# The order of a recorded kernel set anew: local attention and a long convolution on one core

## The chip, the cores and the metric

The kernel runs on one core of a Trainium2 chip. The time is the device time of one execution in microseconds (us), the median of several runs. The profile is one profiled execution, whose span (first to last instruction) is a little shorter than its time.

## What is computed

Two layers over 2048 positions of 576 channels, in bf16, their outputs side by side (1152 channels):

```python
# A: sliding dilated attention, 32 heads of 18 channels, 8 taps, dilation 2
qkv = x @ wqkv
logits[h,s,w] = q[h,s] . k[h,s-2w] * 18**-0.5     # where s-2w >= 0, else -1e9
o = sum_w softmax_w(logits)[h,s,w] * v[h,s-2w]
a = o @ wo
# B: H3 convolution
k_shift[t] = sum_{j<4} k[t-3+j] * shift_k[:, j]
kv = k_shift * v
y = irfft(rfft(pad(kv)) * rfft(pad(ssm_k)))[:2048]   # long causal convolution over time
b = q * (y + kv * ssm_D)
out = concat([a, b], axis=-1)
```

## The kernel before

**How the work is cut.** Everything lives on chip; the two layers are woven into each other. The convolution's transforms are matrix products: the 2048 positions of kv and of the filter are cut into four blocks, each is folded about its middle, multiplied by tables of cosines and sines, multiplied with the filter's spectrum, summed over pairs of blocks and brought back by the inverse tables. The attention projects x to q, k and v by five groups of channels, multiplies q with k shifted by a tap, sums over a head's channels with a matrix of ones, takes the softmax, spreads the weights over the channels by DMA, multiplies with v, and projects with wo.

**What sets the order.** Every piece of work is a job, a function under a short name in the dictionary `jobs`. The scheduler leaves the order alone: the last lines of the kernel (L1090 and L1091) take the names in the string ORDER (L19 to L36) one by one and record each job's instructions. Each engine and each DMA queue then works off its own instructions in the order in which they were recorded, and waits on semaphores for data and for buffers. So ORDER is the order of all engines' queues at once. A name with an apostrophe records a projection with its last channels (the tails) first. PSUM is cut into four slots (`slots`, `banks`, L103 on): a job takes the slot that was given back longest ago, and gives it back, for the order of recording, when its copy out has been recorded. On the chip TensorE waits until that copy is done.

**The names** that the text uses, with their lines in before:

- loads on SyncE's queue: load_x (L178), load_w (L137, L139), load_k (L194, L197, a block of k into a buffer `kj`), load_v (L203, L204, into `vt`), turn_x (L234, L235), Lf0 to Lf3 (the filter, by a transposing DMA, L211), Lk and Lv (k and v of later blocks), Fr (first rows, L578); D0 to D5 spread weights (L789)
- spread_taps (TensorE L449, ScalarE L452 into `skb`): the four taps of shift_k laid out over the partitions
- the tables' angles (VectorE L376, L377) and sines (ScalarE L378)
- turning a quarter of x (TensorE L406, its last 64 channels L411; copies on VectorE L464 and ScalarE L465, L476, tails L416), and project_first (TensorE L435, L437, ScalarE L439)
- T0 to T3: taps of one block (VectorE L513, L516, times v L532). M: folding (TensorE L541, ScalarE L544). k, q and v with two digits or three: projections (TensorE L320, L324, L331, L337, ScalarE L353)
- F: folding the filter (TensorE L598, ScalarE L601, a DMA of POOL's queue L603). K: filter units (TensorE L563, L564, ScalarE L614). x with three digits: the same for kv (L676, L678)
- L: products of q and k (VectorE L700); G: their sums (TensorE L714, ScalarE L718); RG (VectorE L774); sm: softmax (VectorE L738 to L750); V: weights times v (VectorE L808); A: their sums (TensorE L819, L833, ScalarE L822); O: the projection with wo (TensorE L883, L875, ScalarE L889)
- ak and ax: third sums for the product by three multiplications (VectorE L937); p: products of spectra (VectorE L945); z: their sums (TensorE L964, ScalarE L977, for z323 in part VectorE L975); i: inverse (TensorE L999, ScalarE L1002; the last, i3384L, L1018 and L1020); b: back (TensorE L1048, L1027, ScalarE L1054); Q: q's loads on POOL's queue (L927, L929); g: gates (VectorE L1064, the last ones L1009)

**The head.** Until the first name of ORDER, the kernel records its start by plain code: loads of x, k, v and weights, the spread of the taps, four tables, the turning of quarters 0 and 1 of x, and the four project_first.

Of the kernel before, what the change touches and what calls it, by code (L numbers as in the profile page):

```python
# [11 lines left out]
ACT = mybir.ActivationFunctionType  # L12
# [4 lines left out]
PSUM = bass.MemoryType.PSUM  # L17

ORDER = """  # L19
    T0 k00a k00b S1 k01a' k01b I0 k02a k02b k03a' I1 k03b X5 q10a q10b q11a' q11b Lk2 Lv2 T1 q12a q12b M00 q13a'  # L20
    Lk3 Lv3 Lf3 Lf2 Lf1 Lf0 Lw Lo3 Lo2 Lo1 Lo0 Fr Ex T2 q13b k10a k10b M10 k11a' k11b k12a k12b M01 k13a' k13b
    T3 N3 N2 M11 q24a q24b M20 k24a' k24b M21 F3 F2 M30 K310 K311 K312 K313 M31 SV Z2 x000 L000 L001 G000 G001
    L002 N1 N0 L003 x001 x010 F1 G002 G003 L004 L010 x011 K300 K301 K302 G004 G010 L011 L012 K303 K210 K211 K212
    K213 F0 G011 G012 L013 L014 K200 K201 K202 K203 U3 G013 G014 L100 RG0 RG1 sm0a K110 K111 K112 K113 x020 K100
    K101 K102 K103 U2 K010 x021 x030 K011 sm0b L101 K012 K013 v24a v24b G100 G101 L102 K000 K001 K002 K003 sm0c
    L103 G102 G103 sm0d D0 L104 L110 x031 v00a v00b v01a' G104 G110 L111 L112 v01b v02a v02b G111 G112 L113 L114
    v03a' v03b x200 x201 G113 G114 D1 D2 Wl U1 V04 v10a v10b A04 sm1a v11a' sm1b V10 V11 v11b v12a v12b sm1c
    x210 x211 x220 x221 A10 V12 sm1d D3 V13 D4 v13a' v13b x230 A11 V20 V21 x231 x100 x101 x110 x111 A20 V22 V23
    x120 x121 x130 x131 x300 A21 V34 A34 D5 V40 V41 x301 x310 x311 x320 x321 x330 x331 A40 V42 V43 O000 O001'
    A41 V50 V51 O010 O011' A50 V52 V53 O100 O101' A51 Tx2 Tk2 Q0 Q1 ak00 ax00 p000 ak01 ax01 p010 ak02 ax02 p020  # L30
    O110 z000 ak10 p100 O111' O020 z010 ax10 p101 O021' O030 z020 p110 p111 O031' O120 z100 z101 p120 p121 i000
    i02880 z110 z111 p200 p201 i001 i02881 b00 z120 z121 p202 p210 p211 b0288 O121' z200 z201 z202 g0 Q2 p212
    p220 p221 i100 i12880 i101 i12881 b10 z210 z211 z212 p222 ak30 p300 b1288 O130 O131' z220 z221 z222 g1 Q3
    p301 p302 ax30 p303 i200 i22880 i201 z300 z301 p310 p311 z302 z303 p312 p313 i22881 z310 z311 p320 p321 b20
    b2288 z312 z313 p322 p323 g2 i300 z320 z321 i301 z322 z323 b30 i3384L g30 g3384
"""  # L36

LHOMES = (0, 1, 2, 0, 1, 2, 0, 1, 2, 0, 1, 2, 0, 1, 0, 1, 0, 1, 0, 1)
# [11 lines left out]
def kernel(  # L50
# [121 lines left out]

    def kTok(m):
        return view(Ks, k_at(m, 2), [[D, 4], [1, D]])
    kjs, vts = [], []

    def load_x(qtr):
        nc.sync.dma_start(xnat[:, qtr], xf[512 * qtr:512 * qtr + 512, :].rearrange("(sb p) c -> p sb c", p=128))  # L178

    load_x(0)  # L180

    def load_k(i):

        eng = nc.sync
        kj = sp1.tile([128, 7, D], BF16, name="kj", bufs=2)
        r0 = BL * i
        low = [(0, 64)]
        if i == 0:
            nc.gpsimd.memset(kj[0:1, 0:3, :], 0.0)
            nc.gpsimd.dma_start(kj[0:1, 3:7, :], kf[0:4, :].unsqueeze(0))  # L190
            low = [(1, 49), (49, 64)]
        for a, b in ((3, 7), (0, 3)) if i == 0 else ((0, 7),):
            for p0, p1 in low:
                eng.dma_start(kj[2 * p0:2 * p1:2, a:b], bass.AP(  # L194
                    tensor=kf.tensor, offset=kf.offset + (r0 + 4 * p0 - 3 + a) * D,
                    ap=[[4 * D, p1 - p0], [D, b - a], [1, D]]))
            eng.dma_start(kj[1:128:2, a:b], bass.AP(tensor=kf.tensor, offset=kf.offset + (r0 + 256 + 3 - a) * D,  # L197
                                                    ap=[[4 * D, 64], [-D, b - a], [1, D]]))
        kjs.append(kj)

    def load_v(i):
        vt = sp1.tile([128, 4, D], BF16, name="vt", bufs=2)
        nc.sync.dma_start(vt[0:128:2], vf[BL * i:BL * i + 256, :].rearrange("(p c) d -> p c d", c=4))  # L203
        nc.sync.dma_start(vt[1:128:2], bass.AP(tensor=vf.tensor, offset=vf.offset + (BL * i + 256 + 3) * D,  # L204
                                              ap=[[4 * D, 64], [-D, 4], [1, D]]))
        vts.append(vt)

    def load_filter(m):

# [18 lines left out]
    load_w(nc.sync, 0)  # L228
    load_x(1)
# [150 lines left out]
    def table_k(c):  # L380
        return table(n_all[:, 2 * c:2 * c + 2, :], TK[:, c, :, :], n_all[:, 8, :], (2 + c, 2 + c), 2048, (256.0, 1792.0))
# [74 lines left out]
    spread_taps(512)  # L456
    spread_taps(0)
    sines = [table_k(0), table_k(1)]
    pts, held = zip(*[banks("ps_x", BF16) for _ in range(2)])
    for n in range(2):  # L460
        transpose_x(0, pts[n], 2 * n, range(4))
    tail_x(0, pts[1])
    for n in range(2):
        nc.vector.tensor_copy(xT(n, 0, 512), pts[0][:, n, 0:512])  # L464
        nc.scalar.activation(xT(2 + n, 0, 512), pts[1][:, n, 0:512], ACT.Copy)  # L465
    copy_tail(0, pts[1])
    slots.extend(held)
    spread_taps(256)
    sines += [table_x(0), table_x(1)]
    project_first(0, 0)  # L470
    pts, held = zip(*[banks("ps_x", BF16) for _ in range(2)])
    for n in range(2):
        transpose_x(1, pts[n], 2 * n, range(4))
    tail_x(1, pts[0])
    for n in range(2):
        nc.scalar.activation(view(xw, 3 * HB + 2048 * n + 512, [[1024, 2], [1, 512]]), pts[n][:, :, 0:512], ACT.Copy)  # L476
    copy_tail(1, pts[0])
    slots.extend(held)
    project_first(0, 2)
    sines[2]()  # L480
    for n in range(2):
        project_first(1, 2 * n)
        sines[3 - 3 * n]()
    def job(name, fn, *args):

        assert name not in jobs
        jobs[name] = partial(fn, *args)

    project(0, 1)
    project(0, 2)  # L490
    for jj in range(3):
# [142 lines left out]
    for m in range(NBL):  # L634
        job(f"N{m}", negate, m)
        job(f"F{m}", fold_filter, m)
        for cs in range(2):
            for gi in range(4):
                job(f"K{m}{cs}{gi}", filter_unit, m, cs, gi)
        if m:  # L640
            job(f"U{m}", turn_filter, m)
        if m > 1:
            job(f"Lk{m}", load_k, m)
# [479 lines left out]
```

## Time and profile before

| | us |
|---|---|
| median of 3 runs | 210.41 (210.32 to 210.48) |
| profiled execution, its own time | 210.57 |
| its span | 208.9 |
| TensorE busy | 200.0 (96%) |
| VectorE busy | 197.2 (94%) |
| ScalarE busy | 150.5 (72%) |
| POOL busy | 69.7 (33%) |

The granted clock of TensorE is 0.999. 'PE' is TensorE's matmuls, 'PEld' its loads of weights, DVE is VectorE, ACT is ScalarE, SPq the DMA queue of SyncE. A row of the timeline has the start, the busy time from there, the engine, the line and operation, out<-in, how many instructions the row joins, and in brackets the idle time just before with what ended it. A row of the groups has the busy time, the mean ns of one, and the idle time before them.

### The profile page before, as it was taken

To read this page: it belongs to the slowest core of one execution; us is meant where nothing else is said; L and a number is where in the kernel's file an instruction comes from. 1 tells how busy PE (TensorE), PEld (TensorE's weight loads), DVE (VectorE), ACT (ScalarE), POOL (GpSimd) and SP (SyncE) were. 2 spreads that over 40 slices of the span, in tenths; PEclk is the share of its full clock that TensorE was granted. 3 is DMA by queue.
4 is the path that set the end of the run, shared out by engine and by line. 5 is a ranking of instruction groups with operands and counts; after the bars stand their busy time and mean duration, and the time that the engine had idled before them with its cause. 6 is when DMAs were issued, how large, how long until landed. Compare 5 with 4: busy or idle time off the path is not lost.

```text
span 208.9 us, 5092 instructions
## 1 busy us (share of the span) xinstructions
PE 200.0 (96%) x2114; PEld 111.5 (53%) x2122; DVE 197.2 (94%) x150; ACT 150.5 (72%) x218; POOL 69.7 (33%) x104
## 2 busy tenths in 40 slices
PE   7999999999999999999999999999999999999891
PEld 2553344444655567453445465755566667676460
DVE  7989999999999999989899999999999999899982
ACT  3689866967898989965469687954588896764640
POOL 8999992023295095220280000004330001211000
PEclk9999999999999999999999999999999999999999
DMA  6999999999386466999999795789991105454034
GB/s 195 288 295 279 186 283 389 187 215 287 94 113 82 63 82 103 182 172 217 205 238 216 140 242 126 125 208 256 228 287 68 61 3 169 116 169 116 3 108 118
DMA packets 34084, 36.12 MB, mean 173 GB/s; under 512 B 17459, under 2 KB 28847, under 8 KB 34062
## 3 DMA queue, kind: packets, MB, share of 16 engines
q1 hardware_dynamic: 26380, 23.11, 44.7%
q0 software_dynamic: 5216, 10.19, 25.3%
q10 hardware_dynamic: 2466, 2.51, 3.6%
q8 instruction: 16, 0.26, 0.5%
q14 instruction: 6, 0.05, 0.1%
HBM read 13.11 MB, written 4.72 MB: 85 GB/s over the span
## 4 chain that ended last, share of the span: by engine, by line
PE 78%; DVE 10%; issue 5%; ACT 4%; DVEq 0%
PE ps_proj L320 16%; PE ps_wo L883 7%; PE ps_acc L819 6%; PE ps_z L964 6%; PE ps_fx L676 6%; PE ps_inv L999 5%; PE ps_fk L563 4%; PE ps_proj L435 3%; PE ps_log L714 3%; PE ps_proj L331 3%; PE ps_proj L324 3%; DVE qk L945 2%; DVE av L700 2%; PE ps_fk L564 2%; PE ps_fold L541 2%
## 5 line engine op out<-in xcount | busy, mean ns | idle before, releaser
L320 PE MATMUL ps_proj<-xw 128*128 128x512 bf16 x153 | 36.2, 380 | 0.7 <-issue 0.6
L700 DVE TENSOR_TENSOR av<-qk 128x4096 bf16<-128x4096 bf16 (+1 forms) x16 | 31.4, 2012 | 0.0
L320 PEld LDWEIGHTS <-xw 128*128 128x128 bf16 x160 | 14.3, 98 | 19.5 <-issue 4.3
L977 ACT ACTIVATE av<-ps_z 128x768 bf16<-128x768 f32 x23 | 17.4, 809 | 6.2 <-PE ps_z L964 6.2
L678 ACT ACTIVATE xw<-ps_fx 128x576 bf16<-128x576 f32 x32 | 18.9, 676 | 1.8 <-PE ps_fx L676 1.6
L353 ACT ACTIVATE qk<-ps_proj 128x1024 bf16<-128x1024 f32 x14 | 14.3, 1023 | 7.7 <-PE ps_proj L331 4.1
L945 DVE TENSOR_TENSOR qk<-xw,Ks 128x2304 bf16<-128x2304 bf16 x14 | 18.6, 1354 | 1.0 <-PE ps_z L964 0.7
L614 ACT ACTIVATE Ks<-ps_fk 128x576 bf16<-128x576 f32 x32 | 18.9, 718 | 0.8 <-PE ps_fk L564 0.6
L513 DVE TENSOR_TENSOR tB<-kj,skb 128x4608 bf16<-128x4608 bf16 (+1 forms) x8 | 19.3, 2417 | 0.1
L883 PE MATMUL ps_wo<-qk 128*128 128x288 bf16 x128 | 17.9, 287 | 0.0
L676 PE MATMUL ps_fx<-xw,TB 128*128 128x288 bf16 x128 | 17.8, 286 | 0.1
L563 PE MATMUL ps_fk<-Ks,TB 128*128 128x384 bf16 x62 | 16.2, 326 | 0.0
L999 PE MATMUL ps_inv<-av,TI 128*128 128x288 bf16 (+1 forms) x112 | 15.6, 292 | 0.6 <-ACT av L977 0.6
L819 PE MATMUL ps_acc<-av,ident 64*64 64x512 bf16 x160 | 15.3, 379 | 0.0
L564 PE MATMUL ps_fk<-Ks,TB 128*128 128x192 bf16 x62 | 15.2, 246 | 0.0
L676 PEld LDWEIGHTS <-TB 128*128 128x128 bf16 x128 | 12.0, 98 | 5.9 <-issue 2.5
L927 POOL DMA_DIRECT2D TB<-in_B_q_dram x4 | 3.0, 738 | 36.3 <-DVE v L945 23.5
L353 ACT ACTIVATE v<-ps_proj 128x1024 bf16<-128x1024 f32 x9 | 9.2, 1039 | 7.8 <-PE ps_proj L320 4.3
L883 PEld LDWEIGHTS <-qk 128*128 128x128 bf16 x128 | 11.5, 98 | 6.3 <-issue 3.8
L822 ACT ACTIVATE qk<-ps_acc 128x1024 bf16<-128x1024 f32 x8 | 8.2, 1023 | 8.0 <-PE ps_acc L819 8.0
L808 DVE TENSOR_TENSOR av<-Ks,v 128x4096 bf16<-128x4096 bf16 x6 | 13.7, 2287 | 0.0
L622 POOL DMA_DIRECT2D Ks<-Ks x7 | 11.1, 2100 | 7.1 <-ACT Ks L614 6.6
(194 smaller groups left out, 464.6 us busy)
## 6 DMA issues: line engine op xcount, KB each, us to landing
Ks<-Ks POOLq DMA_DIRECT2D x7, 576.0 KB, 8.7
TB<-av SPq DMA_DIRECT2D x12, 256.0 KB, 4.5
kj<-in_B_k_dram SPq DMA_DIRECT2D x6, 504.0 KB, 6.3
vt<-in_B_v_dram SPq DMA_DIRECT2D x8, 288.0 KB, 5.2
Ks<-av SPq DMA_DIRECT2D x8, 256.0 KB, 5.8
out_dram<-qk ACTq DMA_DIRECT2D x5, 288.0 KB, 3.1
Ks<-in_A_x_dram SPq DMA_DIRECT2D x2, 576.0 KB, 5.3
xw<-in_A_wqkv_dram SPq DMA_DIRECT2D x2, 576.0 KB, 6.1
```

The costliest lines, as they stand in the source:

```text
L320: nc.tensor.matmul(ps[:, jp, :], wq(kb, comp, 128 * ct, 128), xT(kb, 1024 * jj + 512 * jp, 512), **se)
L353: nc.scalar.activation(view(t, o + pad + 1024 * jj, [[512, 2], [1, 512]]), ps[:], ACT.Copy)
L513: tt(to, view(kj, row * D, [[D, n], [D, 4], [1, D]]), view(skb, row * D, [[D, n], [0, 4], [1, D]]), ALU.mult)
L563: nc.tensor.matmul(o[:, 0:2], w, rhs[:, 0:2], start=start, stop=stop)
L564: nc.tensor.matmul(o[:, 2], w, rhs[:, 2], start=start, stop=stop)
L614: nc.scalar.activation(view(Ks, k_at(m, cs ^ (m & 1)) + 96 * gi, [[768, 3], [384, 2], [1, 96]]), acc3(ps), ACT.Copy, scale=(PSG, MSG)[cs][ ...
L676: nc.tensor.matmul(ps[:, pm, 0:HD], TX[:, 2 * pm + c, 128 * gi:128 * gi + 128], kv[:, 2 * c + pm, HD * h:HD * h + HD], start=(c == 0), sto ...
L700: tt(view(P, at, [[step, 4], [256, nj], [1, 256]]), view(t, o + 256 * hh, [[0, 4], [512, nj], [1, 256]]), view(tk, ok + 2 + 8 * ug + 256 * ...
L819: nc.tensor.matmul(acc[64 * o:64 * o + 64, h, :], ident[64 * h:64 * h + 64, 64 * h:64 * h + 64], view(P[s], 256 * u, [[2048, 2], [1, 256]] ...
L883: nc.tensor.matmul(ps[:, r, 0:HD], oT(hh, j + 2 * r, t)[:, o:o + 128], wo[:, t // 2, t % 2, HD * h:HD * h + HD], start=(t == 0 and not fli ...
L945: tt(product_home(n), view(xw, HB * XG[i] + QTR * t, [[HB, 3], [1, QTR]]), view(Ks, k_at(j - i, 0) + QTR * t, [[HB, 3], [1, QTR]]), ALU.mult)
L999: nc.tensor.matmul(ps[:, c, 0:n], TI[:, sl, pm, 128 * c:128 * c + 128], Yall(j % 2, pm, sl, slice(c0, c0 + n)), start=(pm == 0 and sl == 0 ...
```

## The change

Three things. The head's work becomes jobs: spread_taps (`sp0`, `sp256`, `sp512`), the tables' angles (`ta0` to `ta3`) and sines (`S0`, `S2`, `S3`, beside S1), the turning of quarter q by halves n (`tqn`), project_first (`pfqn`), and the loads (`LXn`, `LWn`, `LTn`, `Lk0a`, `Lk0b`, `Lvn`, `Lk1`). The kj of block 0 is cleared and its first row loaded on POOL's queue behind the making of `ident`. And ORDER is a new string, from its first name to its last. The number of instructions of each engine stays.

```diff
-    load_x(0)
-    def load_k(i):
+    def load_k(i, part):
...
-    for a, b in ((3, 7), (0, 3)) if i == 0 else ((0, 7),):
+        a, b = ((3, 7), (0, 3), (0, 7))[part]
...
+    kjs[0] = sp1.tile([128, 7, D], BF16, name="kj", bufs=2)
+    nc.gpsimd.memset(kjs[0][0:1, 0:3, :], 0.0)
+    nc.gpsimd.dma_start(kjs[0][0:1, 3:7, :], kf[0:4, :].unsqueeze(0))
...
-    load_k(0)
-    load_w(nc.sync, 1)
-    load_v(0)
-    load_k(1)
-    turn_x(0)
-    turn_x(1)
-    load_v(1)
...
+    def turn_quarter(qtr, n):
+        pt, slot = banks("ps_x", BF16)
+        transpose_x(qtr, pt, 2 * n, range(4))
+        tail = n != qtr
+        if tail:
+            tail_x(qtr, pt)
+        if qtr == 0:
+            for e in range(2):
+                if n:
+                    nc.scalar.activation(xT(2 + e, 0, 512), pt[:, e, 0:512], ACT.Copy)
+                else:
+                    nc.vector.tensor_copy(xT(e, 0, 512), pt[:, e, 0:512])
+        else:
+            nc.scalar.activation(view(xw, 3 * HB + 2048 * n + 512, [[1024, 2], [1, 512]]), pt[:, :, 0:512], ACT.Copy)
+        if tail:
+            copy_tail(qtr, pt)
+        slots.append(slot)
```

ORDER begins in before `T0 k00a k00b S1 k01a' k01b I0`, and in after `LX1 ta0 LX0 sp256 t10 ta2 sp0 sp512 t11 t01 t00 LW0 pf11 Lk0a pf10 Lk0b pf00 LW1 S0 k02a k00a Lk1 ta1 pf01 k03a' Lv0 LT0 ta3 k03b T0`. Quarter 1 is now loaded and turned first.

Where the instructions stand, at three places. ScalarE at the start, behind the load of its tables (`ps_sk` are spread taps, `ps_x` turned x, `ps_proj` projections), in before:

```order
L452 ACTIVATE skb<-ps_sk 128x4x64
L452 ACTIVATE skb<-ps_sk 128x4x256
L465 ACTIVATE xw<-ps_x 128x512 x2
L416 ACTIVATE xw<-ps_x 64x512
L452 ACTIVATE skb<-ps_sk 128x4x256
L439 ACTIVATE qk<-ps_proj 128x2x512
L476 ACTIVATE xw<-ps_x 128x2x512 x2
L416 ACTIVATE xw<-ps_x 64x512
```

and in after:

```order
L440 ACTIVATE skb<-ps_sk 128x4x256
L474 ACTIVATE xw<-ps_x 128x2x512
L404 ACTIVATE xw<-ps_x 64x512
L440 ACTIVATE skb<-ps_sk 128x4x256
L440 ACTIVATE skb<-ps_sk 128x4x64
L474 ACTIVATE xw<-ps_x 128x2x512
L470 ACTIVATE xw<-ps_x 128x512 x2
L404 ACTIVATE xw<-ps_x 64x512
L427 ACTIVATE qk<-ps_proj 128x2x512 x3
```

All copies of turned x now come ahead of the first projection's, with the spread of sp0 and sp512 between the first half of quarter 1 and the rest. On VectorE the copies of t00 stand behind two of the four tables (ta0 and ta2) and ahead of the others, as the copies of quarter 0 did in before.

VectorE in the middle, at the products of weights and v (L808); the last row below is the first product with the weights that D5 spreads into TB. The difference, + for after:

```order
 L808 TENSOR_TENSOR qk<-qk,v 128x4096
+L937 TENSOR_TENSOR xw<-xw 128x768
 L808 TENSOR_TENSOR av<-TB,v 128x4096
+L937 TENSOR_TENSOR xw<-xw 128x768
+L937 TENSOR_TENSOR Ks<-Ks 128x768 x2
+L937 TENSOR_TENSOR xw<-xw 128x768
 L808 TENSOR_TENSOR av<-Ks,v 128x4096
 L808 TENSOR_TENSOR qk<-Ks,v 128x4096
 L808 TENSOR_TENSOR av<-Ks,v 128x4096 x2
 L808 TENSOR_TENSOR qk<-TB,v 128x4096
```

Five third sums have moved from behind these products to between them.

ScalarE at the end (`ps_z` are sums of spectral products, `ps_inv` inverses, `ps_back` the way back, `ps_wo` the attention's output), in before:

```order
L977 ACTIVATE av<-ps_z 128x4x192 x2
L1002 ACTIVATE v<-ps_inv 128x2x288
L1054 ACTIVATE v<-ps_back 128x2x288 x2
L977 ACTIVATE av<-ps_z 128x4x192 x2
L1002 ACTIVATE v<-ps_inv 128x2x384 x2
L977 ACTIVATE av<-ps_z 128x4x192
L1020 ACTIVATE v<-ps_inv 128x2x192 x2
```

and in after:

```order
L977 ACTIVATE av<-ps_z 128x4x192 x2
L1002 ACTIVATE v<-ps_inv 128x2x288
L1002 ACTIVATE v<-ps_inv 128x2x384
L1002 ACTIVATE v<-ps_inv 128x2x288
L1002 ACTIVATE v<-ps_inv 128x2x384
L1054 ACTIVATE v<-ps_back 128x2x288
L977 ACTIVATE av<-ps_z 128x4x192
L889 ACTIVATE TB<-ps_wo 128x2x288
L893 DMA out_dram<-TB 128x2x576
L1020 ACTIVATE v<-ps_inv 128x2x192 x2
```

The inverses of block 2 (288 columns) have moved behind the sums of block 3, and the last output of the attention (O121') stands just ahead of the last inverse. On VectorE the gate g1 has moved from ahead of the products p301 on to behind p313. On SyncE the load of vt for block 3 has moved from ahead of the four filter transposes (L211) to behind three of them.

More of the change, by code (lines that the diff above doesn't have):

```diff
@@ L19 @@
 ORDER = """
[L20 to L34, printed above, removed]
@@ L35 @@
-    b2288 z312 z313 p322 p323 g2 i300 z320 z321 i301 z322 z323 b30 i3384L g30 g3384
+    LX1 ta0 LX0 sp256 t10 ta2 sp0 sp512 t11 t01 t00 LW0 pf11 Lk0a pf10 Lk0b pf00 LW1 S0 k02a k00a Lk1 ta1 pf01
+    k03a' Lv0 LT0 ta3 k03b T0 k02b LT1 M00 k01a k01b Lv1 T1 Lk2 M01 Lv2 k00b Lk3 X5 T2 Lf3 N3 S3 q24a k13a k13b
+    q10a' q10b q24b Lo3 q11a' S1 Lf0 S2 q11b Lf1 Lv3 Lf2 k10a' k10b M10 Fr k12a' k12b I0 k11a F3 T3 N2 Ex k24a
+    k24b k11b M21 q12a' K311 q12b Lo1 N0 q13a' q13b x011 K312 x021 K300 Lo0 K303 SV L001 Z2 Lo2 F2 K313 M20 x000
@@ L36 @@
+    i02881 O120 b0288 z210 p221 z211 z212 p222 ax30 z220 z221 z222 b00 ak30 i12880 i200 p303 Q0 g0 i100 i201
+    i101 i12881 p300 z300 p301 b1288 p302 p310 b20 z301 b10 p311 z302 p312 z303 Q2 p313 O131 z310 z311 z312 z313
+    g1 p322 p321 i22880 i300 p320 i22881 p323 i301 b2288 z320 z321 g2 z322 z323 O121' b30 i3384L Q3 g30 g3384
 """
```

87 lines of the change are left out of this document (41 added, 46 removed).

## The prediction

> **What bounds the kernel now.** I read the page's busy times and the chain that ended last first, then the idle gaps on VectorE's timeline, then the two places where the new order changes most, the start and the end.
>
> ```profile
> PE 200.0 (96%) x2114; PEld 111.5 (53%) x2122; DVE 197.2 (94%) x150; ACT 150.5 (72%) x218; POOL 69.7 (33%) x104
> PE 78%; DVE 10%; issue 5%; ACT 4%; DVEq 0%
> ```
>
> The first line is busy time and share of the span (208.9 us), the second the chain of waits by engine. TensorE is busy for 200.0 us and VectorE for 197.2, so both are nearly full, and no order can take away more than the few us that are left. Instruction counts are the same after the change (2122 matmuls, 150 VectorE operations), so the change can only move waits, the cost of switching between kinds of matmul, and the two ends where one engine has no work. The ends of matmuls are modelled, so I take VectorE's gaps as the account; here are all of 0.3 us and more behind the start (start, busy time, engine, line, operation, and in brackets the idle time ahead with what ended it):
>
> ```profile
> 12.08 1.36 DVE L513 TENSOR_TENSOR xw<-kj,skb 128x2304 bf16<-128x2304 bf16 x1 [0.94 <-DMA kj<-in_B_k_dram]
> 91.38 1.23 DVE L750 TENSOR_TENSOR av<-av 128x2048 bf16<-128x2048 bf16 x1 [0.62 <-ACT av L758]
> 104.83 2.29 DVE L808 TENSOR_TENSOR av<-TB,v 128x4096 bf16<-128x4096 bf16 x1 [1.12 <-PE ps_log L714]
> 139.98 2.29 DVE L808 TENSOR_TENSOR qk<-TB,v 128x4096 bf16<-128x4096 bf16 x1 [0.35 <-DMA TB<-av]
> 178.59 1.36 DVE L945 TENSOR_TENSOR qk<-xw,Ks 128x2304 bf16<-128x2304 bf16 x1 [0.71 <-PE ps_z L964]
> 201.51 0.96 DVE L975 CAST av<-ps_z 128x768 bf16<-128x768 f32 x1 [0.90 <-PE ps_z L964]
> 204.57 1.02 DVE L1009 TENSOR_TENSOR TB<-ps_back,TB 128x384 bf16<-128x384 f32 x2 [0.78 <-PE ps_back L1027]
> ```
>
> VectorE runs without a gap of 0.3 us from 12.08 to 91.38, waits 0.62 + 1.12 + 0.35 + 0.71 = 2.80 us in the middle, and from about 194 on it follows TensorE. The span is therefore: when T0, the first tap job, starts (12.08), plus VectorE's work, plus the middle waits, plus TensorE's last stretch. I forecast these one by one, against the profiled execution's own 210.57 us (208.9 span and 1.7 around it), which lies 0.16 above the median of 210.41.
>
> **The head.** VectorE's rows, then TensorE's, then ScalarE's:
>
> ```profile
> 4.13 0.88 DVE L376 TENSOR_SCALAR Ks<-Ks,rp 128x512 int32<-128x512 int32 x2
> 5.05 0.69 DVE L377 TENSOR_SCALAR Ks<-Ks 128x1024 int32<-128x1024 int32 x1
> 7.23 0.75 DVE L464 COPY xw<-ps_x 128x512 bf16<-128x512 bf16 x2
> 10.39 0.75 DVE L377 TENSOR_SCALAR Ks<-Ks 128x1024 int32<-128x1024 int32 x1
> ```
> ```profile
> 2.98 2.31 PE L449 MATMUL ps_sk<-tB,ones 97*128 97x256 bf16 x6
> 5.09 1.91 PE L406 MATMUL ps_x<-ident,Ks 128*128 128x128 bf16 x16
> 8.16 1.89 PE L435 MATMUL ps_proj<-xw 128*128 128x512 bf16 x8
> 10.52 1.07 PE L406 MATMUL ps_x<-ident,Ks 128*128 128x128 bf16 x16
> ```
> ```profile
> 8.36 0.58 ACT L416 ACTIVATE xw<-ps_x 64x512 bf16<-64x512 bf16 x1
> 8.84 1.02 ACT L452 ACTIVATE skb<-ps_sk 128x1024 bf16<-128x1024 f32 x1
> 11.96 1.94 ACT L476 ACTIVATE xw<-ps_x 128x1024 bf16<-128x1024 bf16 x2 [0.32 <-PE ps_x L411]
> ```
>
> In before, VectorE's two copies of the turned quarter 0 (0.75, from 7.23) stand between four sine tables of about 1.57 each (0.88 + 0.69), two ahead and two behind; the tables end at 10.39 + 0.75 = 11.1, and T0 waits 0.94 more for kj. In after the same two tables stand ahead and two behind, but the copies now belong to t00, the last of four transposing jobs instead of the first. Step by step: the quarter loaded first is now quarter 1, with the same place and size on SyncE's queue, so its transposes start at about 5.1. t10 has 8 + 4 transposes at 1.91/16 = 0.12, about 1.25 us, to 6.35. ScalarE turns them over with 1.94/2 = 0.97 and 0.58, one behind the other, to about 7.6. Behind these in ScalarE's queue stands the copy of sp0 (1.02), to about 8.6, and t00 takes the bank that sp0 frees, since the four banks go round in the order of the jobs. t00's eight transposes (0.5 at the later 1.07/16) and two semaphore steps end at about 9.45. Then VectorE has 0.75 + 2 x 1.57 = 3.9 to do: T0 starts at 13.3 and not at 12.08. kj, which was late at 12.08, keeps its place on the queue and is covered. **Term: +1.2 us**, between +0.5 (if t00 does not wait for sp0's bank: 9.45 - 0.7) and +1.7.
>
> The transposes ran at 107 ns a piece until about 7.0 (1.91 for 16) although TensorE had been busy since 1.27 us. The Trainium skill, "TensorE: Matmul & The Clock Gate", section "What's actually happening", gives the full clock after about 3.4 us of sustained work, which would be 4.7 here. By that rule t10's twelve transposes would be 0.5 us shorter and the time would come to 210.3; the trace disagrees, with full speed only past 5 us of work, and the measurement decides.
>
> TensorE's first projection starts at about 10.0 (8.16 before), but one group of 20 transposes (10.52 to 11.86) that was behind it is now ahead: TensorE stands some 0.6 to 1.0 later through the head. Up to 60 us I count this as covered, since VectorE does not wait for TensorE there.
>
> **The middle.** Three things change for VectorE. The softmax's first wait (0.62 at 91.38, for ScalarE) stays, at about 0.7. The wait of 0.35 at 139.98 is for a DMA that spreads the weights; the change puts five small third_sum operations (768 columns each) ahead of that row, which cover it. The waits of 1.12 at 104.83 and 0.71 at 178.59 are for TensorE; in the new order the log sums and the spectral sums stand earlier against VectorE's work, with 0.1 to 0.9 us to spare by the durations of before. New waits of about 0.45 in all arise at two score products (L012, L014) and at sm0a. So 2.80 becomes about 1.15. **Term: -1.65 us**, between 0 (every wait comes back elsewhere) and -2.8. Four waits of about 0.1 ahead of filter products go as well: **-0.2**.
>
> What that costs TensorE:
>
> ```profile
> 16.06 0.60 PE L437 MATMUL ps_proj<-xw 64*128 64x512 bf16 x2
> 16.59 1.90 PE L435 MATMUL ps_proj<-xw 128*128 128x512 bf16 x8
> 18.43 0.60 PE L437 MATMUL ps_proj<-xw 64*128 64x512 bf16 x2
> ```
>
> Two tail matmuls of 512 columns take 16.59 - 16.06 = 0.53 and eight full ones 18.43 - 16.59 = 1.84; at x a matmul and y a change of tile shape, 2x + y = 0.53 and 8x + y = 1.84, so a matmul is 0.218 and a change 0.09. There are 130 such changes in the order of before and 137 in that of after: 7 x 0.09 = +0.65 us on TensorE. Filter units now stand mostly in a row:
>
> ```profile
> 58.45 2.34 ACT L614 ACTIVATE Ks<-ps_fk 128x576 bf16<-128x576 f32 x4
> ```
> ```profile
> 57.23 0.34 PE L563 MATMUL ps_fk<-Ks,TB 128*128 128x384 bf16 x1
> ...
> 59.12 0.25 PE L564 MATMUL ps_fk<-Ks,TB 128*128 128x192 bf16 x1
> ```
>
> ScalarE empties one in 2.34/4 = 0.585, and TensorE fills one in about 0.49 (the two rows are the first and the last of sixteen, four units in 59.2 - 57.23 = 1.97). A row of eight such units leaves ScalarE 8 x 0.095 = 0.76 behind; three spare banks of 0.49 cover that once. Around F2, M20 and F1 (57 to 64 us) they don't, and I find about 1 us of waiting for banks. Both costs go on TensorE, 1.65 in all with no term of the sum, because the spare time against VectorE (0.1 to 0.9) and the tail's work, taken out of the middle below, cover them in the likeliest case. If that cover is gone they cost up to 1.65.
>
> On SyncE, the load of v's last part (vt) now stands behind three of the four filter transposes:
>
> ```profile
> 34.82 13.83 SPq L211 DMA_TRANSPOSE Ks<-in_B_ssm_k_dram  x4
> ```
> ```profile
> vt<-in_B_v_dram SPq DMA_DIRECT2D x8, 288.0 KB, 5.2
> ```
> ```profile
> 53.51 1.36 DVE L532 TENSOR_TENSOR xw<-xw,vt 128x2304 bf16<-128x2304 bf16 x1
> ```
>
> Each transpose holds the queue for 13.83/4 = 3.5 us, so vt is issued at about 34.8 + 10.4 or a little earlier, at 44 to 45, and lands by 50.5 (5.2 from issue to landing, the median of these loads in the second row); T3 multiplies by it at 53.51 before and about 1 us later now. Nothing, with 4 us to spare.
>
> **The tail.** VectorE's row, then TensorE's:
>
> ```profile
> 194.18 1.35 DVE L945 TENSOR_TENSOR av<-xw,Ks 128x2304 bf16<-128x2304 bf16 x1
> ...
> 199.25 1.35 DVE L1064 TENSOR_TENSOR TB<-v,TB 128x2304 bf16<-128x2304 bf16 x1
> ```
> ```profile
> 180.01 1.15 PE L883 MATMUL ps_wo<-qk 128*128 128x288 bf16 x8
> 181.09 0.44 PE L875 MATMUL ps_wo<-qk 64*64 64x288 bf16 x8
> ...
> 190.40 1.15 PE L999 MATMUL ps_inv<-av,TI 128*128 128x288 bf16 x8
> 191.48 0.36 PE L964 MATMUL ps_z<-av,ident 64*64 64x384 bf16 x4
> ...
> 194.31 0.36 PE L964 MATMUL ps_z<-qk,ident 64*64 64x384 bf16 x4 [0.20 <-DVE qk L945]
> 195.74 1.46 PE L999 MATMUL ps_inv<-av,TI 128*128 128x384 bf16 x8 [0.58 <-ACT av L977]
> 197.13 0.36 PE L964 MATMUL ps_z<-av,ident 64*64 64x384 bf16 x4
> ...
> 198.56 1.47 PE L999 MATMUL ps_inv<-av,TI 128*128 128x384 bf16 x8
> ...
> 202.04 1.48 PE L1018 MATMUL ps_inv<-av,TI 128*128 128x192 bf16 x16 [0.26 <-ACT av L977]
> ```
>
> In before the product p313 ends at 194.18 (TensorE's row at 194.31 waits for it), and the last gate g3384 starts at 204.57: 10.39 us. In after TensorE has this behind p313: z313 0.75 with its wait, i22880 1.0 (190.40 to 191.48, less the change of shape), i300 1.3 (195.74 to 197.13, less the same), i22881 1.0 and 0.2 of waiting for ScalarE, i301 1.3, b2288 0.25, z320 to z323 four times 0.67 (two of them and a change stand between 197.13 and 198.56), O121' 1.3 (1.08 and 0.38 in the rows at 180.01 and 181.09, less a change, as its tails come first), b30 0.4, and i3384L 2.5 to the end (202.04 to 204.57): 12.7 us, 2.3 more than 10.39. But p313 comes earlier: gate g1 (1.35 - 0.08 of overlap, row 199.25 is one of its kind) has moved from ahead of it to behind it, which gives 1.3 back. **Term: +1.0**, between 0 (TensorE's earlier work was in the way of p313 as well) and +2.3 (p313 gains nothing). Q3's load, which must wait for g1's stores, is issued late, but i3384L still hides it.
>
> **Sum:** +1.2 - 1.65 - 0.2 + 1.0 = +0.35: the profiled execution goes from 210.57 to 210.9, and the median from 210.41 to **210.8**.
>
> **Rivals.**
> (A) *The middle gives all and the head costs less.* With T0 at 12.6 (+0.5) and 2.8 gone in the middle instead of 1.65, the sum is 0.5 - 2.8 - 0.2 + 1.0 = -1.5, so 208.9; with about half of what that gains over the forecast, 209.7. For it: every middle wait has a named cause that the order treats. Against it: TensorE is at 96%, and a wait it loses at one place has come back at the next one all along the chain (78%).
> (B) *TensorE becomes the bound, on the other side.* The 0.65 of changes of shape and 1 us of bank waits meet a slack against VectorE of 0.1 to 0.9; from the point where TensorE's delay passes 0.9, the rest goes into VectorE's waits at the log sums (104.83) one for one. Then the middle gains 0 to 0.8 and not 1.65, and the time is 210.8 + 0.85 to 210.8 + 1.65, so 211.6 to 212.4. For it: the busy shares and the later first projection. That changing the tile shape drains TensorE is also what the Trainium skill, "TensorEngine Tiling (Array Packing)", section "Key Properties", says; the trace agrees, with 0.09 us for each.
> (C) *A transfer is late:* vt behind the transposes, or Q3's load behind g1's stores. It decides from 4 us more than I reckon; then 213 and over.
> (D) *The order matters nowhere,* since both engines were full anyway: 210.4, which lies in the forecast's band.
>
> **How the numbers follow.** Forecast and D, 210.0 to 211.1: 0.40. A, 208.5 to 210.0: 0.30. B, 211.1 to 212.5 and somewhat over: 0.25. C: 0.05. A difference of 0.2% (209.99 to 210.83) is about what measuring this kernel can tell from no change: of the forecast's 0.40, 0.27 lies within it and 0.13 above. So faster 0.30, same 0.27, slower 0.13 + 0.25 + 0.05 = 0.43. The range of 208.9 to 212.5 leaves out the deepest of A (0.06), the top of B (0.06) and C (0.05). The likeliest case's own range is 210.0 to 211.1.
>
> **What the changed profile would show.** The head is right if the first row of the tap products starts at 13.3 with no wait for kj but right behind the tables, and wrong if it starts before 12.6. The middle is right if VectorE's gaps between 14 and 190 sum to about 1.2, with none for the spread DMA at V50. B holds if they sum to over 2.5 with TensorE as releaser. The tail is right if p313's end and the last gate lie 12.7 apart. The prediction is wrong if a gap of over 1 us stands at a place that I have not named.

## The result, and the profile after

The changed kernel takes 211.45 us (median of 20 runs, 210.27 to 213.63), the kernel before 210.31 in the same session (20 runs): a ratio of 1.0053 with a 95% interval of 1.0034 to 1.0073. It is slower by half a percent, 1.1 us. The forecast was 210.8, 0.35 us slower by its sum. The range of 208.9 to 212.5 holds the time, but the likeliest case's own band (210.0 to 211.1) does not: 211.45 lies in the band of rival (B). The sum is short by some 0.7 us, and the runs show that two of its steps were wrong in opposite directions.

The profiled execution took 211.37, its span is 209.7 against 208.9. Busy times and chain of the changed kernel's page:

```profile
PE 200.0 (95%) x2112; PEld 112.1 (53%) x2122; DVE 196.5 (94%) x150; ACT 151.1 (72%) x218; POOL 62.3 (30%) x104
PE 61%; DVE 16%; issue 9%; DMA 7%; ACT 3%; SPq 1%; DVEq 0%
```

The engines do the same work. New in the chain are 7% of DMA, which it did not list before. VectorE's gaps of 0.3 us and more behind 9 us, with the first tap product (13.52) and the gate g1 (192.06):

```profile
9.78 0.76 DVE L472 COPY xw<-ps_x 128x512 bf16<-128x512 bf16 x2 [2.46 <-PE ps_x L394]
...
13.52 1.36 DVE L513 TENSOR_TENSOR xw<-kj,skb 128x2304 bf16<-128x2304 bf16 x1
...
143.32 2.29 DVE L808 TENSOR_TENSOR qk<-TB,v 128x4096 bf16<-128x4096 bf16 x1 [1.69 <-DMA TB<-av]
...
192.06 1.35 DVE L1064 TENSOR_TENSOR TB<-v,TB 128x2304 bf16<-128x2304 bf16 x1
...
199.67 1.36 DVE L1064 TENSOR_TENSOR TB<-v,TB 128x2304 bf16<-128x2304 bf16 x1 [1.20 <-ACT v L1054]
...
205.36 1.02 DVE L1009 TENSOR_TENSOR TB<-ps_back,TB 128x384 bf16<-128x384 f32 x2 [1.47 <-PE ps_back L1027]
```

T0 starts at 13.52 (12.08 before). In the middle a single wait is left, for the DMA at V50: it grew from 0.35 to 1.69, and all the others are gone. g1 at 192.06 marks p313's end; from there to the last gate it is 205.36 - 192.06 = 13.3 us. TensorE waits once for VectorE behind the late V50 and then has no wait until 0.21 us, for ScalarE, at the way back of the last inverse:

```profile
149.13 0.40 PE L819 MATMUL ps_acc<-av,ident 64*64 64x512 bf16 x2 [1.14 <-DVE av L808]
...
204.88 0.27 PE L1027 MATMUL ps_back<-v,ident 64*64 64x192 bf16 x2 [0.21 <-ACT v L1020]
```

So behind 149 us TensorE is full, and what delays V50 by more than TensorE still has to do moves the whole end. Why is the DMA late? SyncE's queue in before, then SyncE's and POOL's in after; L789 is the spread D5, L630 and the first L622 behind 130 us are Tx2 (a copy, then an addition by DMA), the pair of L622 is U1, and each DMA of L622 or L630 moves 576 KB:

```profile
130.82 3.55 SPq L789 DMA_DIRECT2D TB<-av  x4
134.47 1.45 SPq L630 DMA_DIRECT2D xw<-xw  x1
```
```profile
128.37 0.52 SPq L630 DMA_DIRECT2D xw<-xw  x1
130.75 3.73 SPq L789 DMA_DIRECT2D TB<-av  x4
```
```profile
132.06 1.23 POOL L622 DMA_DIRECT2D xw<-xw  x1 [24.98 <-ACT xw L678]
132.81 2.91 POOL L622 DMA_DIRECT2D Ks<-Ks  x2
```

D5 goes out at the same time in both (130.8). In before nothing large stands ahead of it: Tx2's copy goes out behind it, U1 had gone out at 106. In after Tx2's copy is under way already when D5 goes out, and three more large DMAs start within 3 us of it. D5's last piece is issued at about 134.4 in both; it has landed by 139.9 before and by 143.3 after.

### The profile page after: what moved, and what is told of

The parts are those of the page before. It is cut to its first block, busy times and chain, and to the rows that moved or that the text cites. A ratio compares the mean times of both kernels' runs of the same rounds, so it can differ in the third digit from the quotient of the medians.

```text
span 209.7 us, 5082 instructions
## 1 busy us (share of the span) xinstructions
PE 200.0 (95%) x2112; PEld 112.1 (53%) x2122; DVE 196.5 (94%) x150; ACT 151.1 (72%) x218; POOL 62.3 (30%) x104
## 4 chain that ended last, share of the span: by engine, by line
PE 61%; DVE 16%; issue 9%; DMA 7%; ACT 3%; SPq 1%; DVEq 0%
PE ps_proj L308 14%; PE ps_z L964 10%; PE ps_inv L999 7%; DVE av L808 5%; DVE av L700 5%; PE ps_wo L883 5%; DMA TB<-av 5%; PE ps_proj L423 3%; PE ps_acc L819 3%; PE ps_fx L676 3%; PE ps_proj L319 3%; PE ps_log L714 2%; DMA Ks<-in_A_x_dram 2%; PE ps_rev L598 2%; PE ps_fold L541 2%
## 5 line engine op out<-in xcount | busy, mean ns | idle before, releaser
L308 PE MATMUL ps_proj<-xw 128*128 128x512 bf16 x151 | 37.1, 380 | 1.1 <-issue 0.6
L945 DVE TENSOR_TENSOR qk<-xw,Ks 128x2304 bf16<-128x2304 bf16 x14 | 18.6, 1349 | 0.0
L676 PE MATMUL ps_fx<-xw,TB 128*128 128x288 bf16 x128 | 18.6, 287 | 0.0
L622 POOL DMA_DIRECT2D Ks<-Ks x7 | 10.4, 1645 | 24.5 <-DMA Ks<-Ks 19.6
L676 PEld LDWEIGHTS <-TB 128*128 128x128 bf16 x128 | 11.4, 98 | 7.6 <-issue 4.4
L808 DVE TENSOR_TENSOR av<-Ks,v 128x4096 bf16<-128x4096 bf16 x6 | 13.6, 2287 | 0.1
```

The costliest lines, as they stand in the source:

```text
L308: nc.tensor.matmul(ps[:, jp, :], wq(kb, comp, 128 * ct, 128), xT(kb, 1024 * jj + 512 * jp, 512), **se)
L676: nc.tensor.matmul(ps[:, pm, 0:HD], TX[:, 2 * pm + c, 128 * gi:128 * gi + 128], kv[:, 2 * c + pm, HD * h:HD * h + HD], start=(c == 0), sto ...
L808: tt(view(weight_home(n, ct), 0, [[2048, 2], [256, W], [1, 256]]), view(t, at, [[step, 2], [256, W], [1, 256]]), view(late["v"], voff + 2 ...
```

## The experiments

All ratios are against the kernel before, in the same session (its median was 210.21 for d5_clear, u1_early, old_head and new_head, 210.43 for the other runs up to d5_loaded, 210.11 for the rest); where it helps, a run is compared with the changed kernel's 211.45. In the names of jobs a diff shows what moved in ORDER.

**1. D5 cleared of both, and of U1 alone.**

```diff
 d5_clear, u1_early:  -V50 O101 U1 x121   +V50 O101 x121     -x320 Wl ax01   +x320 Wl U1 ax01
 d5_clear only:       -ak02 Tx2 O000      +ak02 O000         -D5 x301        +D5 Tx2 x301
```

> The changed kernel, with U1 put behind Wl (its DMAs then go out near 106 us) and Tx2 put behind D5, both as the order of before has them. Theory 1 (traffic: D5's landing is late because Tx2 and U1, four DMAs of 576 KB, share the DMA engines with it from 128 to 144 us): the wait of 1.69 us ahead of the fourth-but-last weight product falls to 0 to 0.4 us and the time falls by 1.0 to 1.6 us, to 209.9 to 210.5, and runs scatter less than the 210.3 to 213.6 of the changed kernel. Theory 2 (TensorE is the bound behind 149 us, whatever VectorE waits): the wait goes, the time falls by less than 0.4 us. Theory 3 (D5 is late by itself, since its four DMAs replicate by reading twice): the wait stays at over 1.2 us.

> The changed kernel with U1 alone put behind Wl; Tx2 stays ahead of D5. U1 is two of the four DMAs of 576 KB beside D5. Theory 1 (traffic): the wait ahead of the weight product falls to 0.4 to 1.0 us and the time by 0.6 to 1.2 us. Theory 2 (TensorE bound): time within 0.4 us of the changed kernel's. Theory 3 (D5 late by itself): the wait stays at over 1.2 us.

d5_clear: 211.33 us, ratio 1.002 (0.9989 to 1.0052). But its twelve runs lie in two groups, five at 209.1 to 209.8 and seven at 211.1 to 212.0. u1_early: 210.88, ratio 1.0043 (1.0018 to 1.0068), eight at 210.2 to 211.0 and four at 211.5 to 213.0. In d5_clear VectorE has no wait at V50 any more; in u1_early it is

```profile
142.18 2.29 DVE L808 TENSOR_TENSOR qk<-TB,v 128x4096 bf16<-128x4096 bf16 x1 [1.17 <-DMA TB<-av]
```

The load on the DMA engines is seen in the table by stretches (us; busy time of PE, PEld, DVE, ACT, POOL with the instructions; granted clock, share of the DMA engines, GB/s). These are the 2 us ahead of D5's first issue and the 4 us behind it, first of after (issue at 130.75), then of d5_clear (132.65):

```profile
128.75:130.75 2.00, 2.00 (x31) 1.12 (x24) 2.00 (x2) 1.33 (x3) 0.00 (x0) 1.00 0.62 256
130.75:134.75 4.00, 4.00 (x62) 2.71 (x61) 4.00 (x6) 2.77 (x6) 2.69 (x3) 1.00 0.76 142
```
```profile
130.65:132.65 2.00, 2.00 (x31) 1.11 (x24) 2.00 (x2) 1.33 (x3) 0.00 (x0) 1.00 0.00 0
132.65:136.65 4.00, 4.00 (x62) 2.71 (x61) 4.00 (x6) 2.77 (x6) 0.00 (x0) 1.00 0.70 124
```

The traffic theory holds in the direction and the wait: D5 is issued to idle DMA engines (busy 0.00 in the 2 us ahead of it instead of 0.62), from then on they are about equally busy (0.70 and 0.76) but in after with the other transfers too, and D5's wait is gone. The time of the lower group fell by 1.9 us, from 211.4 (median of the changed kernel's fourteen runs under 212) to 209.5. Over all runs the two medians are nearly the same (211.45 and 211.33), so the gain has to be read within a group here; experiments 3 and 4 have pairs without an upper group, and they give 1.4 and 1.7 us. The theory of a slow D5 by itself falls, and with these pairs so does that of TensorE as the bound whatever VectorE waits. u1_early alone would not decide: its wait of 1.17 and its gain of 0.57 us lie between the ranges of the theories. The upper group of d5_clear was expected by none of them. Its profiled execution belongs to it, and shows where it comes from: T0 starts not at 13.5 but at

```profile
15.45 1.43 DVE L513 TENSOR_TENSOR xw<-kj,skb 128x2304 bf16<-128x2304 bf16 x1
```

TensorE's weight loads at the start, in u1_early and in d5_clear (the first row of each is t10's eight transposes, d5_clear's last is t11 and t01):

```profile
4.90 0.45 PEld L394 LDWEIGHTS <-Ks 128*128 128x128 bf16 x8 [0.94 <-DMA Ks<-in_A_x_dram]
```
```profile
4.89 0.77 PEld L394 LDWEIGHTS <-Ks 128*128 128x128 bf16 x8 [0.93 <-DMA Ks<-in_A_x_dram]
...
8.33 1.86 PEld L394 LDWEIGHTS <-Ks 128*128 128x128 bf16 x16
```

In one execution eight take 0.45 us already at 4.9, in the other sixteen still take 1.86 at 8.3, and full speed comes only behind 10.4. The clock column says 1.00 in both, so it does not show this; the durations do.

**2. The start alone, both ways.**

```diff
 old_head:  -LX1 ta0 LX0 sp256 t10 ta2 sp0 sp512 t11 t01 t00 LW0 pf11 ...
            +LX0 LW0 LX1 Lk0a Lk0b LW1 Lv0 Lk1 LT0 LT1 Lv1 sp512 sp0 ta0 ta1 t00 t01 sp256 ta2 ta3
            +pf00 t10 t11 pf01 S2 pf10 S3 pf11 S0   (then the rest of after's order)
 new_head:  after's start, ahead of T0 and the whole order of before
```

> The changed kernel with its start in the order of before: quarter 0 loaded and turned first, all turning, tables, sines and first projections ahead of T0. Theory 1 (head carried on: VectorE is the bound from T0 to the softmax): T0 starts at 12.0 to 12.4 instead of 13.5, every later row of VectorE moves with it, and the time falls by 1.0 to 1.5 us. Theory 2 (TensorE absorbs it): T0 starts early, but the gain is met by waits of VectorE in the middle or by the same wait for D5, and the time falls by less than 0.5 us.

> The order of before with the start of the changed kernel ahead of T0 (quarter 1 turned first, t00 last). Theory 1: T0 starts at 13.3 to 13.7, and the time rises by 0.8 to 1.5 us over before, since VectorE has no gap to lose it in up to 91 us. Theory 2 (the middle waits of before, 0.62 and 1.12 us, take it up, because they are for ScalarE and TensorE, which run on): the time rises by 0 to 0.5 us.

old_head: 210.55 (210.09 to 211.18), ratio 1.0015 (1.0002 to 1.0027): T0 at 11.76, and 0.9 us less than after, just under the first theory's 1.0 to 1.5 and over the second's 0.5. Part of the 1.76 us gained at T0 came back as a wait of 0.40 at the softmax; the wait for D5 stayed at 1.49. new_head: 211.99 (210.99 to 213.31), ratio 1.0086 (1.0057 to 1.0115), 1.8 us slower than before, more than the 0.8 to 1.5 expected; its profiled execution (211.62) is one of the faster. That profile has T0 at 13.35 and the three middle waits of before for ScalarE and TensorE unchanged (0.64, 1.12, 0.72): they took up nothing. Only D5's 0.35 is gone. So the start is carried on to the end. And the wide scatter goes with the new start: after, new_head, d5_clear and u1_early spread over 2.3 to 3.4 us, old_head over 1.1. (It is not the only source of scatter: d5_loaded below, with the old start, spreads over 3.7.)

**3. The clock at the start.** Ahead of the first transposes TensorE's weight loads pause for 0.9 to 1.3 us in the runs with the new start and four idle matmuls (0.62 in before), since four matmuls of the taps stand there and not six. That is the row of the loads. The matmuls' row, with its modelled ends, has a pause of only 0.04 to 0.57 us there, and none in before, so the "gap of 0.96 us" of the expectation below is one of the loads.

```diff
-    idle_work(4)
+    idle_work(6)
```

> The changed kernel with six idle matmuls at the start instead of four, which fill TensorE's gap of 0.96 us ahead of the first transposes. Theory (clock): the runs fall into two groups 1.5 to 2 us apart (210.3 to 211.8 and 212.5 to 213.6) because the full clock opens at 5 to 7 us in some executions and at 10.4 in others, when the gap falls into the window that decides; without the gap the upper group is gone, all runs lie at 210.3 to 211.9, and the median is 211.0 to 211.4. Rival (the groups come from DMA traffic at D5): two groups stay, with 3 in 10 of the runs at 212.5 or over.

> The changed kernel with U1 behind Wl, Tx2 behind D5 and six idle matmuls. d5_clear had five runs at 209.1 to 209.8 and seven at 211.1 to 212.0, with the matmuls cold until 10.4 us in the profiled one of the upper group. Theory (clock): with the gap filled all runs lie at 209.1 to 210.0. Rival (the groups come from something else): about half of the runs stay at 211 or over.

warm6: 211.42 (210.73 to 212.3), ratio 1.0053 (1.0034 to 1.0072); d5_clear_warm6: 210.02 (209.1 to 210.67), ratio 0.9986 (0.9967 to 1.0005). The upper groups are gone in both (none of 24 runs there; 6 of 20 and 7 of 12 without the filling), which speaks for the clock and against the DMAs as the cause of the groups. Whether the pause itself decides is not shown: among the profiles without the filling, new_head has the longest pause (1.28) and its transposes run at full speed from the start, and the two idle matmuls also add work. Nor did the filling make the kernel faster: warm6's median is that of after (211.42 against 211.45), and the runs did not all go to the bottom: they spread evenly over 1.6 us, wider than expected for d5_clear_warm6. What the pair does give, without groups, is the price of the traffic: 211.42 less 210.02 is 1.4 us. In the profiled execution of d5_clear_warm6 full speed comes within the first eight transposes (0.83 us of TensorE from 5.52 us on, against 0.62 in u1_early and 1.03 in after), and T0 starts at 13.81. The instant at which full speed comes still differs between executions, from under 4.9 to 7.0 us in the profiles without a late clock, and t00 waits for it. A run cannot choose that instant, so this much was not tested further.

**4. Both causes away.**

```diff
 clear_old_head:  old_head, and U1 and Tx2 as in d5_clear
```

> The changed kernel with the start of before, U1 behind Wl and Tx2 behind D5: two of the causes taken away at once. If the head and the traffic at D5 each cost what the runs so far suggest (0.8 for the start, 1.6 for the traffic, from 211.3 in the changed kernel's lower group of runs), the time is 208.8 to 209.4, under before's 210.2, with runs within 1 us of each other. If both only uncover the same bound (TensorE behind 149 us), it is 209.4 to 210.2.

208.83 us, ratio 0.9932 (0.9907 to 0.9957), seven runs within 0.08 us of each other. That is the lower edge of what was expected if both causes count, 2.6 us below after and some 1.5 below before: the rest of the new order is good. Against old_head, which has the same start, the two names moved give 210.55 less 208.83, so 1.7 us, with no groups in either. The page's busy times and VectorE's gaps of 0.3 us and more from 8 to 190 us:

```profile
PE 200.4 (97%) x2122; PEld 112.3 (54%) x2122; DVE 196.7 (95%) x150; ACT 151.3 (73%) x218; POOL 67.7 (33%) x104
```
```profile
12.08 1.36 DVE L513 TENSOR_TENSOR xw<-kj,skb 128x2304 bf16<-128x2304 bf16 x1 [0.92 <-DMA kj<-in_B_k_dram]
...
86.87 1.23 DVE L750 TENSOR_TENSOR av<-av 128x2048 bf16<-128x2048 bf16 x1 [0.40 <-ACT av L758]
```

Of the middle's 2.80 us of before, 0.40 is left. T0 starts as in before; 2.4 us less in the middle, 1.0 less between dependent operations (experiment 7) and 1.6 more in the tail (13.30 from p313's end to the last gate, as in after) make 1.8 us less, against 1.7 by the spans (208.9 and 207.2).

**5. The traffic put into before, and Tx2 alone.**

```diff
 d5_loaded (order of before):  Tx2 ahead of D5, U1 behind V50
 tx2_late (after):             Tx2 behind D5, U1 stays behind V50
```

> The order of before, with Tx2 ahead of D5 and U1 behind the weight product V50, as the changed kernel has them; nothing else moved. Theory (traffic): the wait for the spread weights grows from 0.35 to 1.3 to 2.5 us and the time by 0.8 to 1.6 us, to 211.0 to 211.8. Rival (D5 lands late in the changed kernel for another reason, or TensorE covers it): the wait stays under 0.8 us and the time within 0.4 us of before's.

> The changed kernel with Tx2 alone put behind D5 (U1 stays late). d5_clear, with both, gained about 1.6 us against the changed kernel in runs of the same group; u1_early 0.55. If the two add up, Tx2 alone gives 0.8 to 1.2 us: the lower group at 210.1 to 210.6, the wait for the spread weights 0.3 to 0.9 us. If what counts is that SyncE's copy goes out ahead of D5 on the same queue (so that U1 is harmless once it is behind), it gives all of 1.6: 209.4 to 210.0, no wait.

d5_loaded: 216.01 (214.48 to 218.19), ratio 1.0265 (1.0219 to 1.0311), far more than the 0.8 to 1.6 expected:

```profile
143.49 2.29 DVE L808 TENSOR_TENSOR qk<-TB,v 128x4096 bf16<-128x4096 bf16 x1 [3.92 <-DMA TB<-av]
```

D5 lands at the same 143.4 as in after, but the order of before has no third sums between the weight products, so VectorE comes to V50 at 139.6 and waits 3.92, 3.6 more than before. The rest comes by way of TensorE, which stood idle for the products and then ran slower (its rows, and the stretch of 2 us with the lowest granted clock, the last figure but two):

```profile
145.83 0.40 PE L819 MATMUL ps_acc<-qk,ident 64*64 64x512 bf16 x2 [1.65 <-DVE qk L808]
148.03 0.40 PE L819 MATMUL ps_acc<-av,ident 64*64 64x512 bf16 x2 [1.80 <-DVE av L808]
```
```profile
150.00:152.00 2.00, 2.00 (x13) 0.79 (x7) 1.71 (x2) 1.02 (x1) 1.18 (x1) 0.50 0.29 84
```

The granted clock is 0.73, 0.50 and 0.92 in the three stretches of 2 us from 148 on, which is 1.7 us of TensorE's full speed lost, and VectorE waits for TensorE behind it (0.29 at 150.47, 0.34 at 174.49, 1.52 instead of 0.71 at 183.72). All six runs have a mean granted clock of 0.984 to 0.991. So the 5.6 us are not the price of the traffic alone: a wait that emptied TensorE cost the clock as well. In after the wait left TensorE idle for 1.14 us, and the clock column stays at 1.00. There the five third sums had cut the wait to 1.69: they covered what the prediction said, and the landing was later than it said. tx2_late has no wait at V50, as in d5_clear: 211.32 (209.59 to 213.01), with four runs at 209.6 to 210.3. Its profiled execution is one with the late clock (T0 at 15.61). POOL's queue shows why U1 does no harm there:

```profile
144.59 1.23 POOL L622 DMA_DIRECT2D xw<-xw  x1 [35.45 <-DMA xw<-xw]
145.35 4.14 POOL L622 DMA_DIRECT2D Ks<-Ks  x3
```

U1 stands behind Tx2's addition on POOL's queue, and that waits for Tx2's copy, which SyncE now sends behind D5. One name moved holds all four large DMAs back; the second of the two expectations was right in the wait, and in the time for these four of the twelve runs.

**6. The tail, and kj.**

```diff
 tail_early (clear_old_head):  -z323 O121' b30   +z323 b30     -p313 O131 z310   +p313 O131 O121' z310
 kj_first (clear_old_head):    -LX0 LW0 LX1 Lk0a Lk0b   +LX0 LW0 Lk0a Lk0b LX1
```

> clear_old_head (208.83) with the attention's last output O121' moved from the tail to behind O131, before the last sums. The prediction's step (O121' behind p313 costs TensorE 1.3 us that would be idle time before): the time falls by 0.5 to 1.3 us. Rival (TensorE has no gap from the last weight product to the end, so any order of its jobs is worth the same): within 0.2 us of 208.83, or up to 0.2 slower by changes of tile shape.

> clear_old_head (208.83) with quarter 1 of x (LX1) loaded behind k's first block, so that kj, for which T0 waits 0.92 us, is issued 0.6 us earlier. If VectorE's start carries on to the end: T0 at 11.1 to 11.6, time 208.0 to 208.5. Rival (TensorE's late transposes of quarter 1, or its full queue behind 140 us, take it up): T0 earlier, time within 0.2 us of 208.83 or slower.

tail_early: 209.14 (209.12 to 209.46), ratio 0.9952 (0.9935 to 0.9969): 0.3 us slower, not 0.5 to 1.3 faster, although its T0 starts 0.4 us earlier in the profile (11.68). The output that moved forward holds up the sums, and VectorE now waits for them (this file's lines stand one further down):

```profile
191.68 1.36 DVE L946 TENSOR_TENSOR qk<-xw,Ks 128x2304 bf16<-128x2304 bf16 x1 [0.83 <-PE ps_z L965]
```

kj_first: 212.86 (211.47 to 213.25), ratio 1.0113 (1.0084 to 1.0141), 4 us slower than clear_old_head. (The profiled execution is the fastest, 211.47 at a granted clock of 0.999; the four runs of 212.8 and more have 0.986 to 0.992, so part of the 4 us may be the clock; no profile shows where.) T0 did start at 11.06, but quarter 1 of x, issued behind two loads of k, came 2.6 us later at TensorE than in clear_old_head (12.83 instead of 10.24), and the delay came back at 64.77 on VectorE:

```profile
12.83 0.45 PEld L394 LDWEIGHTS <-Ks 128*128 128x128 bf16 x8 [3.09 <-DMA Ks<-in_A_x_dram]
```
```profile
11.06 1.35 DVE L513 TENSOR_TENSOR xw<-kj,skb 128x2304 bf16<-128x2304 bf16 x1
...
64.77 3.43 DVE L700 TENSOR_TENSOR av<-qk 128x4096 bf16<-128x4096 bf16 x2 [3.40 <-ACT xw L678]
```

**7. Pairs on VectorE.** In before, a product (L945) that follows directly on the third sum (L937) it reads starts 1.45 us behind it. In after the product that stands behind the same third sum (ak10) is p101, which does not read it, and starts 1.27 us behind it:

```profile
155.85 1.35 DVE L937 TENSOR_TENSOR Ks<-Ks 128x2304 bf16<-128x2304 bf16 x1
157.30 1.36 DVE L945 TENSOR_TENSOR qk<-xw,Ks 128x2304 bf16<-128x2304 bf16 x1
```
```profile
157.80 1.35 DVE L937 TENSOR_TENSOR Ks<-Ks 128x2304 bf16<-128x2304 bf16 x1
159.07 1.35 DVE L945 TENSOR_TENSOR av<-xw,Ks 128x2304 bf16<-128x2304 bf16 x1
```

```diff
 spaced (order of before):
-ak00 ax00 p000 ak01 ax01 p010 ak02 ax02 p020
+ak00 ax00 ak01 ax01 ak02 ax02 p000 p010 p020
-z000 ak10 p100 O111' O020 z010 ax10 p101      +z000 ak10 ax10 p100 O111' O020 z010 p101
-p222 ak30 p300    +ak30 p222 p300      -p302 ax30 p303    +ax30 p302 p303
```

> The order of before with the third sums (ak, ax) taken from directly ahead of the product that reads them to one or two operations earlier; nothing else. Theory (an operation of VectorE that reads what the one just ahead wrote starts 0.1 to 0.2 us later; seven such pairs in before, one in the changed kernel): steps of 1.40 to 1.46 us become 1.27, VectorE reaches the sums of the second block 0.5 to 0.8 us earlier, and the time falls by up to 0.8 us if VectorE is the bound there, or by under 0.3 us if its wait for TensorE at p222 (0.71) grows by the same. Rival (the extra is waiting for TensorE's buffers): the steps stay.

The steps became 1.27 as the theory says:

```profile
155.73 1.35 DVE L937 TENSOR_TENSOR Ks<-Ks 128x2304 bf16<-128x2304 bf16 x1
157.00 1.35 DVE L937 TENSOR_TENSOR xw<-xw 128x2304 bf16<-128x2304 bf16 x1
...
181.24 1.36 DVE L937 TENSOR_TENSOR Ks<-Ks 128x2304 bf16<-128x2304 bf16 x1 [2.82 <-PE ps_z L964]
```

The time did not fall: 212.69 (212.22 to 212.89), ratio 1.0113 (1.0094 to 1.0133). The last row is ak30, which I had moved one place ahead: it writes where sums of TensorE still read, and waits 2.82 us, 2.1 more than p222 there before. T0 also started later in this profile (12.91). So the run shows the step and not what the step is worth by itself.

## Why the prediction came out as it did

Each term against the profiled executions:

| step | predicted | measured |
|---|---|---|
| T0's start | +1.2 (13.3) | +1.44 (13.52) |
| named middle waits | -1.65 (2.80 to 1.15) | -1.11 (2.80 to 1.69) |
| four waits ahead of products | -0.2 | about -1.0 |
| tail | +1.0 (12.7, less 1.3 for g1) | +1.6 (13.3 - 10.39, less 1.27) |
| sum | +0.35 | +1.0; span +0.8 |

The terms are read from different rows and leave 0.2 over. They missed by +0.2, +0.5, -0.8 and +0.6, so that the forecast came as near as it did is in part luck: the third of these took off 0.8 of the 1.3 us that the others add up to.

**The head was right in its mechanism**: t00 last, behind sp0's bank, VectorE idle 2.46 us for it, and kj covered. t00's copies start at 9.78 instead of 9.45. (Its 107 ns a transpose is not what its row gives: 1.91 us for 16 is 119 ns, the 0.12 that the sum does use.) What the prediction did not have is that this start is not one number. By the Trainium skill, "TensorE: Matmul & The Clock Gate", section "What's actually happening", the full clock comes after a window of about 3.4 us in which TensorE was busy, and the windows run freely, whenever the kernel starts; I wrote that the trace disagrees, from one execution in which it came at 7.0. The later profiles show t10 at full speed at 4.9 (u1_early), 3.6 us behind the first matmul, in agreement with the page, and in d5_clear and tx2_late only behind 10.4 and 10.5, some 3.4 us later than the 7.0 of before. With the page's window that is what a window with too little work in it, ahead of the transposes, would give; experiment 3 supports this in that two more idle matmuls took the late group away, but the window itself was not seen, and neither was what makes it fail. The price is up to 2 us at T0 (15.45), since in the new order T0 hangs on forty transposes and in the old one on the first twenty.

**The step that failed is the one at V50**: "five small third_sum operations ... which cover it". They were to take the wait there from 0.35 to nothing; it measured 1.69, the whole of what is left in the middle, and by the prediction's own sign (no gap for the spread DMA at V50) its middle was wrong. It held the landing of D5 fixed, and looked at what stands beside the loads of vt and Q3, but not here. The new order put Tx2 ahead of D5 and U1 beside it, and D5 landed 3.4 us later. d5_clear, tx2_late and d5_loaded show that cause from three sides, and clear_old_head against old_head its price, 1.7 us. It was a case of rival (C), a late transfer, at a place that (C) did not name and well under its price, because the third sums did cover 2 us of it.

**The other middle waits were all too dear.** I expected 0.7 at the softmax and 0.45 at L012, L014 and sm0a; there were none of 0.2 us or more. VectorE arrived there later by the late T0, which would cover them: in old_head, with the early T0, 0.40 comes back at the softmax. In this order a late start and the waits behind it can't be added as if they were independent; in the order of before they could, as new_head shows, whose waits stayed.

**The 0.2 for four waits was a misreading.** Those were not waits for TensorE but the step between two operations of which the second reads the first: seven pairs in before, 0.11 to 0.2 each, about 1.1 us, and one in after (0.12). Spacing them is worth 1.0 us of VectorE's time to the changed kernel; spaced shows the step but, by a fault in its own order, not the gain in the end.

**The tail's sum was near in size, wrong in its reason.** 12.7 was predicted and 13.3 measured, but p313 was not what the end waited for: TensorE was full from 149 us on, so work of TensorE moved from ahead of p313 to behind it is the same work. tail_early bears this out: with O121' back ahead of the sums clear_old_head got slower by 0.3 us, not faster. In the tail a gap of over 1 us also stands at a place that the prediction did not name (1.20 at 199.67, for the copy out of b2288), which by its last sentence is a sign against it; the way to the last gate goes over TensorE there, so it cost nothing that the rows show. **Rival (B)**, TensorE as the bound, was half right: from 149 us on it is (and in before too TensorE shows no wait between 131 and 194 us), but (B)'s sign, VectorE's gaps over 2.5 us with TensorE as releaser, is not there: they sum to 1.69, for a DMA. The changes of tile shape and the filter rows cost VectorE nothing that the gaps show. That the time fell into (B)'s band was for other reasons than (B)'s.

## What to carry to other kernels

When an order is changed, list for each DMA that something waits for what else is on the DMA engines from its issue to its landing, on every queue; here two names cost 1.7 us although the waited-for transfer was issued at the same instant. Put work that has to start early behind as little cold TensorE work as possible, and look at the durations for the instant of full speed. Idle matmuls at the start took the slowest runs away here, and left the median where it was. A wait that empties TensorE in mid-kernel can cost more than itself: the clock fell behind it in d5_loaded. And try the parts of a new order apart: this one held 1.5 us of gain over the kernel before, hidden under a start and a transfer that cost 2.6.

## What the runs showed of the hardware that was not expected

- The same transposes' weight loads took 0.45/8 = 56 ns each at 4.9 us in one execution and 1.86/16 = 116 ns at 8.3 us in another, while the profile's line of the granted clock reads full in both. In mid-kernel the line did show a drop: to 0.50 from 150 to 152 us in d5_loaded, behind idle times of 1.65 and 1.80 us.
- Two operations of VectorE in a row, the second reading the first's output, are 1.40 to 1.46 us apart for 2304 columns, against 1.27 for independent ones.
- D5's four DMAs of 256 KB landed 5.5 us after the last was issued in before, with one transfer of 576 KB issued behind them, and 8.8 us after it in the changed kernel, with one issued 2.4 us ahead and three beside them.
